# A two-layer recurrent-memory transformer on one core: sums and value products in column tiles, and an order for each of four segments

## The chip, the core and the metric

The kernel runs on one core of a Trainium2 chip. The metric is the device time of the whole launch in microseconds (us). TensorE is called PE here, VectorE DVE, ScalarE ACT, GpSimd POOL, SyncE SP. PE multiplies a loaded (stationary) block of weights with a moving operand. It can be used as one array of 128 x 128 ("full") or as four column tiles of 128 x 32 that work on outputs in four groups of 32 partitions ("col"). A row of the profile that says `128*128` is a full matmul, one that says `128*32` a matmul in one column tile. PE writes to eight PSUM banks, from which ACT and DVE copy results out.

## The reference

The input has 2048 tokens of width 512. Two kinds of layer alternate, A B A B, each on a layer norm (LN) of the running sum and added to it.

```python
def _A_ref(x, mem0, Wq, Wk, Wv, Wo, seg_len):        # 32 heads of 128, seg_len 32, M = 8
    mem = mem0
    for s in range(n_seg):                            # 64 segments, one after the other
        h = concatenate([mem, x[:, s*seg_len:(s+1)*seg_len]], axis=1)     # 40 rows
        q, k, v = h @ Wq, h @ Wk, h @ Wv              # per head
        p = softmax(where(mask, q @ k.T * scale, -1e9))
        o = (p @ v) @ Wo                              # summed over heads
        mem = o[:, :M]                                # goes into the next segment
        outs.append(o[:, M:])

def _B_ref(x, wqkv, wo):                              # 32 heads of 16, linear attention
    q, k, v = split(x @ wqkv)
    pq, pk = phi(q), phi(k)                           # phi(t) = t+1 or exp(t), + 1e-6
    kv, z = pk.T @ v, sum(pk)                         # over all 2048 tokens
    return ((pq @ kv) / (pq @ z + 1e-6)) @ wo
```

The `mask` is causal among the tokens of a segment; its first eight columns, the memory, are seen by all rows.

## The kernel before, in words

**Tiling.** The tokens are 16 tiles of 128 rows; a tile has four segments of 32 tokens. For each segment (`a_layer`, the loop over `s` from L1190) the operand `hT` holds 8 memory rows and 24 of the 32 tokens, so a block has 32 columns and fits a column tile. The last eight tokens of each segment ("left") are gathered for the four segments of a tile and projected together, once a tile (`left_block`, L857). `project` (L786) makes half of the 32 heads at a time: four k-blocks, each with four matmuls in the four column tiles, 512 columns each. The halves are called b = 0 and b = 1. Keys and queries are then turned by transposes on PE (L815) or by a DMA transpose on SP's queue (L806).

**One segment.** In order: keys, queries and values for both halves; scores of the memory queries and all others (`mem_attention`, L916: L936 and L942), Exp on ACT (L953), a masking product on DVE (L963), the sums over keys (L969: a matmul with ones, so that every partition gets the sum), the inverse of the sum as Exp of -Ln (L972, L974), the products with values (L979 for the left keys, L982 for the others), the scaling on DVE (L986). Then `out_block` projects with Wo (L1084), and `next_mem` (L1109) makes the next segment's memory rows. That loop is the recurrence. The attention of the segment's own tokens (`x_attention`, L991: sums at L1014 and L1018, products with values at L1050 and L1054) needn't be finished for the next memory; its output joins the next segment's output projection.

**Layer B** runs beside it: `b_in` (L1236) takes a finished tile's LN (transposes at L764), projects (L1246, L1280) and accumulates kv and z (L1258, L1264); `b_mid` combines them with the output weights; `b_out` (L1327) applies them (L1349, L1357), while the second A layer runs, and once more at the end. `prepare` (L905) makes the LN of the next tile for layer A.

**Modes before.** Projections, transposes of keys and queries, scores, L1014, L1018, L1084 and L1109 are `mode="col"`. L969, L979, L982, L1050, L1054 and the matmuls of layer B and of LN have `mode="full"`, the default of `add`.

**What sets the order.** The program is a list of nodes; `schedule` (L221) walks a modelled time and gives each engine its next node, so every engine's instruction order is fixed when the kernel is built. Semaphore waits follow from the dependencies. A node's priority comes from a written table, OFFSET, by the name of its step and its number in it:

```python
nd.prio = -(step * PERIOD + OFFSET[name][k])
```

Here `step` is the segment number. The higher priority goes first. On PE the mode counts too (L344 to L353): the node of highest priority is set aside in favour of a ready node of the present mode, unless that one's priority is lower by more than MODE_SLACK; a switch is charged PE_SWITCH = 0.1 us in the plan. LOOK (L356) lets PE hold back when a node of higher priority becomes ready within that time. A node that is not urgent also has to leave PSUM banks free for urgent ones.

The function `at` (L780) names the step: the plain name for most segments, with `F` at the first of a layer and `L` at the end. `c_pe` and `c_pe4` (L110 to L115) are the plan's costs of full and of column matmuls.

Of the kernel before, what the change touches and what calls it, by code (L numbers as in the profile page):

```python
# [19 lines left out]
MODE_SLACK = 257.520800  # L20

LOOK = 0.037900

PERIOD = 13.5
# [6 lines left out]
    "startF": (-180.90,),  # L31
    "prepF": (-121.35, 60.85, -338.25, -337.90, -107.00, -87.50, -299.25, -329.00, -408.50, 3.85, -143.55),
    "left0F": (-363.40, -329.55, -494.35, -352.10, 94.85, -208.40, -136.40, -396.90, -232.20, -403.00, -128.90,
        -405.80, -148.00, -295.50),
    "left1F": (-209.80, -257.05, -186.90, -154.30, -433.85, 6.40, -172.20, -140.25, -80.85, -9.85, -9.35, -386.50,
        -138.50, 95.25),
    "leftv0F": (-372.65, -364.30, -359.05, -256.70, -165.10, -31.45, -453.65, -169.80, -349.15),
    "leftv1F": (11.05, -371.15, -43.60, -159.70, -312.30, -127.00, -348.85, -412.35, -37.50),
    "leftsF": (152.10, -203.75, -335.15, -313.60),
    "xlF": (-408.90,),  # L40
    "k0F": (-374.05, -352.95, -109.35, -38.25, -357.80, -283.65, -389.25),
    "k1F": (-384.40, -311.20, -269.15, -445.45, -358.65, -231.45, 6.45),
    "q0F": (-231.35, -263.70, -41.50, -77.50, -422.45, -255.85, -244.15),
    "q1F": (-403.90, -236.15, -154.40, -217.85, -201.95, 40.05, -395.10),
    "v0F": (-150.70, -57.40, -88.00, -91.90, -412.95),
    "v1F": (-398.50, -281.20, -428.10, -152.00, -135.45),
    "qlF": (-276.35, -262.00),
    "mem0F": (144.85, -273.95, -326.25, -10.00, -100.65, -352.15, -184.30, -65.00, -152.00, -199.90),
    "mem1F": (143.65, -361.45, -383.05, -187.15, -362.20, -392.75, -272.00, -305.00, -257.25, -132.25),
    "warm": (-58.15,),  # L50
    "outF": (-106.90, -344.50, -302.90, -95.35, -235.60, -405.55, -256.55, -367.55, -76.60, -394.15),
    "nextF": (-363.25, 27.95, -353.90),
    "xF": (-185.90, -377.55, 14.75, -293.55, -309.80, -426.90, -378.30, 31.70, -109.50, -293.25, -82.35, -367.45,
        -244.60, -240.60, -354.70, -77.85, -232.55, -363.15, -367.00, -361.35, 25.20, -367.30, 44.65),
    "k0": (-398.40, -409.05, -373.85, -369.85, 132.45, -419.80),
    "k1": (-365.35, -358.40, -356.75, -359.10, -107.85, -297.25, -150.20),
    "q0": (-362.10, -361.85, -360.10, -360.10, -210.50, -303.20, -149.75),
    "q1": (-355.65, -305.05, -346.50, -363.20, -182.55, -219.85, -25.65),
    "v0": (-95.30, 11.05, -162.10, -296.90, -355.00),
    "v1": (-86.30, -164.30, -100.90, 16.15, -110.55),  # L60
    "ql": (-65.10, 8.65),
    "mem0": (-95.60, -319.85, -382.80, -364.30, -364.60, -238.25, -382.75, -409.25, -242.75, -363.50),
    "mem1": (-383.00, -337.30, -215.20, -155.05, -146.75, -237.10, -384.30, 73.95, -107.50, -247.10),
    "out": (-133.90, -320.25, -243.80, -151.90, -140.55, -192.85, -130.00, -224.85, -109.70, -359.70),
    "next": (-146.50, -384.40, -71.35),
    "res": (-183.00, 64.70, -297.70, -251.95, -411.00, -412.55, -365.55, -304.60, -304.65, -295.30, -246.05,
        -110.55, -74.25, -19.80, -371.90),
    "x": (-109.05, -31.75, 114.50, -203.10, -411.65, -359.40, -250.75, -429.60, -384.75, -272.75, -52.30, -225.80,
        -224.30, -229.40, -102.00, -5.70, 33.60, -84.35, -151.60, -296.60, -389.35, -9.55, -276.50),
    "prep": (-19.30, -365.40, -305.25, -166.00, -378.25, -251.70, -384.90, -194.75, -380.20, -282.75, 77.85),  # L70
    "left0": (32.80, -324.50, -411.15, -307.75, -358.90, -202.25, -79.65, -207.35, -187.55, -161.70, -154.90,
        -304.30, -258.10),
    "left1": (-122.95, -119.30, -37.50, -257.65, 25.80, 45.20, -304.15, -368.35, -295.60, -220.55, -372.95,
        -155.60, -281.60),
    "leftv0": (-150.60, -87.70, -74.05, -89.65, 87.70, -306.35, -427.50, 74.20),
    "leftv1": (-93.05, -335.75, -148.00, -153.60, -355.55, -48.40, 175.80, -359.40),
    "lefts": (15.65, -231.70, -259.75, -320.50),
    "xl": (-368.40,),
    "bi": (-160.30, -165.65, -384.40, -460.85, -352.00, -423.00, -276.75, -132.25, -251.60, -360.20, -121.05,
        -144.60, -284.90, -386.70, -405.60, 165.25, -301.95, -305.30, -356.70, -156.05, -73.25, -115.15, 25.75,  # L80
        37.60, -11.70, -163.20, 100.35, -134.80, -166.80, -114.00, -147.35, -398.65),
    "k0L": (-245.45, -353.50, -300.20, -334.30, -361.55, -384.65, -370.40),
    "k1L": (-342.20, -303.05, -383.70, -269.65, -361.15, -244.35, -335.50),
    "lr": (-341.45, -312.30, -306.75, -164.75, -284.05, -386.00, -357.55, -334.15, -416.50, 161.80, -67.40,
        -334.55, -56.15),
    "xL": (154.80, -139.25, -428.60, -145.30, -313.00, -200.15, -368.90, -369.95, -367.85, -432.15, -360.25, 65.65,
        -193.75, -336.60, -371.50, -220.70, -310.95, -427.55, -78.15, -373.70, -404.65),
    "outL": (-183.35, -223.20, -247.40, -365.15, -74.00, -380.60, -56.90, -223.50, -345.60, -38.20),
    "resL": (-280.85, -402.40),
    "biL": (-330.50, -308.55, -333.35, -91.15, -389.95, -228.15, -76.30, -32.45, -294.50, -121.05, -167.60,  # L90
        -377.75, -262.40, -270.20, -25.45, -14.60, -313.50, 59.95, -373.25, -319.65, -43.90, -426.45, -404.80,
        159.50, 90.55, -275.05, -114.60, -274.80, -0.20, -245.85, -186.45, -160.00),
    "bm": (-410.80, -480.25, -344.35, -394.70, -170.00, -356.70, -6.85, 40.95, -34.25, 28.70, -27.10, -86.70, 81.00),
    "boF": (-189.35, -384.50, -486.20, -152.40, -345.90, -400.30, -157.90, -333.20, -255.25, -380.60, -218.45),
    "bo": (-354.35, -361.60, -26.00, -195.25, -364.05, -132.50, 137.45, -348.35, -267.60, -258.70, -358.25),
    "ldL": (-68.35, -367.55),
    "boL": (-254.80, -187.90, -323.40, -61.20, -302.90, -321.15, -73.00, -462.70, -32.35, -155.00),
    "boZ": (-401.60, -128.20, -116.30, -62.60, -31.35, -177.45, -365.75, -28.05, -77.75, -79.45),
# [15 lines left out]
def c_pe(n_mm, n):  # L114
    return n_mm * max(0.0335, (n / 2.4 + 3.0) * 1e-3)  # L115
# [390 lines left out]
def _build_kernel(nc, A_x, A_mem0, A_Wq, A_Wk, A_Wv, A_Wo, A_seg_len, B_wqkv, B_wo, out):  # L506
# [110 lines left out]
    add = P.add  # L617
# [156 lines left out]
    LATE = ("x", "k0", "k1")  # L774

    def a_layer(base, first):
# [3 lines left out]
        def at(s, name):  # L780

            early = s <= 0 or (name[:4] == "left" and not by_dma(s))
            P.at(base + s, name + ("F" if early else "L" if s >= NSEG or (s == NSEG - 1 and name in LATE) else ""))
# [132 lines left out]
        def mem_attention(s, b):  # L916
# [50 lines left out]
            def sums(pe):  # L967
                for a in range(2):
                    r = pe.matmul(tl.f32()[:, 256:384], one_sb[:, :], Pm[:, k, a, :], start=(a == 0), stop=(a == 1))  # L969
                return r  # L970
            add("pe", sums, c_pe(2, 128), reads=[("Pm", k, 0), ("Pm", k, 1), "one"], tiles=[tl], urgent=True)
# [6 lines left out]
            def pvm(pe):  # L978
                pe.matmul(pv.f32()[:, 0:128], vleft[:, g2, b, g, :], Pm[:, k, 1, :], start=True, stop=False)  # L979
                for i, hh in enumerate(hhs):  # L980
                    o = slice(32 * i, 32 * i + 32)
                    r = pe.matmul(pv.f32()[:, o], vimg[:, r2, 128 * hh:128 * hh + 128], Pm[:, k, 0, o], start=False,  # L982
                                  stop=i == 3)
                return r
            add("pe", pvm, c_pe(4, 32) + c_pe(1, 128), reads=[("Pm", k, 0), ("Pm", k, 1), ("v", r2, b), ("vl", g2, b)], tiles=[pv], urgent=True)
# [5 lines left out]
        def x_attention(s):  # L991
# [50 lines left out]
            for b in range(2):  # L1042
                pv = P.tile()
                for i in range(4):

                    def pvx(pe, i=i, b=b, pv=pv):
                        hh = 4 * b + i
                        o = pv.f32()[:, 128 * i:128 * i + 128].rearrange("p (j q) -> p j q", j=4)
                        e = slice(128 * hh, 128 * hh + 128)
                        r = pe.matmul(o, vimg[:, r2, e], Pbx[:, hh, :, :], start=i == 0, stop=False,  # L1050
                                      skip_group_check=True)
                        if i == 3:
                            o = pv.f32()[:, :].rearrange("p (n q) -> p n q", q=32)[:, :, 24:32]
                            r = pe.matmul(o, vleft[:, g2, b, g, :], Pbl[:, b, :], start=False, stop=True,  # L1054
                                          skip_group_check=True)
# [363 lines left out]
```

## Time and profile before

| | us |
|---|---|
| median of 3 runs | 1759.76 |
| lowest, highest | 1757.05, 1760.36 |
| the profiled execution's own time | 1759.18 |
| its span, first to last instruction | 1757.0 |
| PE busy (matmuls) | 1671.6 |
| PE weight loads busy | 1098.7 |
| DVE busy | 1133.8 |
| ACT busy | 1130.2 |
| POOL busy | 329.3 |

The mean granted clock of PE was 0.993 of full speed. In the timeline's rows, the first column is the start from the beginning of the span, the second the time from the first start to the last end of the group, then engine, line, what is written and read, weights and moving operand, and the number of instructions. In brackets is the idle time before it and what ended that. Matmuls overlap: a row's duration contains the latency of its last matmul, so the pace of PE is read from one start to the next. In the list of waits the numbers are total us, times, and the longest.

### The profile page before, as it was taken

How to read it: one execution, taken by the hardware profiler on the slowest of the kernel's cores; microseconds unless marked ns; L12 is line 12 of the kernel's file. 1: busy time of each engine (PE TensorE's matmuls, PEld its weight loads, DVE VectorE, ACT ScalarE, POOL GpSimd, SP SyncE). 2: the span in 40 equal slices, each digit the busy share in tenths (PEclk: the TensorE clock that was granted, in tenths of full speed). 3: DMA queues.
4: the chain of work that ended last, by engine and by line, in shares of the span. 5: the costliest groups of instructions: out<-in, count | busy, mean ns of one | idle time of the engine just before them, and what ended most of it. 6: DMA issues, size and time to landing. Idle time of an engine off the chain costs nothing.

```text
span 1757.0 us, 101000 instructions
## 1 busy us (share of the span) xinstructions
PE 1671.6 (95%) x46027; PEld 1098.7 (63%) x46027; DVE 1133.8 (65%) x3960; ACT 1130.2 (64%) x3069; POOL 329.3 (19%) x660
## 2 busy tenths in 40 slices
PE   5999999999999999999799999999999999999997
PEld 2666666666666666666466666666666666666663
DVE  2566666666666666666555666667666766666657
ACT  3666666666666666666466666666666666666665
POOL 2022221112221111222102221122221112221120
PEclk9999999999999999999999999999999999999999
DMA  9222222212222222222012222122222222222223
GB/s 378 77 37 45 46 45 43 50 39 46 45 41 46 45 47 40 47 50 39 22 25 40 47 47 54 36 52 48 42 52 48 42 45 48 47 47 48 51 68 105
DMA packets 228540, 97.47 MB, mean 55 GB/s; under 512 B 207096, under 2 KB 222256, under 8 KB 226576
## 3 DMA queue, kind: packets, MB, share of 16 engines
q1 hardware_dynamic: 204784, 58.64, 17.8%
q0 software_dynamic: 21744, 19.78, 5.1%
q10 hardware_dynamic: 1584, 12.58, 1.7%
q8 instruction: 360, 5.90, 1.4%
q14 instruction: 68, 0.56, 0.1%
HBM read 29.63 MB, written 10.49 MB: 23 GB/s over the span
## 4 chain that ended last, share of the span: by engine, by line
PE 80%; DMA 8%; DVE 5%; ACT 5%; issue 1%; POOL 1%; ACTq 0%; DVEq 0%
PE pb L793 42%; PE pb L1084 14%; PE pb L815 4%; PE pb L1050 4%; DMA arena_sb<-arena_sb 4%; PE pb L1246 3%; DMA dx_sb<-y_sb 2%; PE pb L936 2%; DVE arena_sb L623 2%; PE pb L1280 2%; PE pb L969 1%; ACT arena_sb L622 1%; DMA Wk_sb<-in_A_Wk_dram 1%; PE pb L1109 1%; PE pb L764 1%
## 5 line engine op out<-in xcount | busy, mean ns | idle before, releaser
L622 ACT ACTIVATE arena_sb<-pb 128x512 bf16<-128x512 f32 (+6 forms) x1375 | 674.3, 509 | 302.6 <-PE pb L793 223.4
L638 POOL DMA_DIRECT2D dx_sb<-y_sb x504 | 256.8, 516 | 1095.6 <-DVE y_sb L1120 485.0
L793 PE MATMUL pb<-Wk_sb,arena_sb 128*32 128x512 bf16 x5120 | 346.7, 382 | 16.5 <-DVE arena_sb L623 6.5
L793 PE MATMUL pb<-Wv_sb,arena_sb 128*32 128x512 bf16 x5120 | 354.0, 379 | 1.7 <-issue 1.6
L793 PE MATMUL pb<-Wq_sb,arena_sb 128*32 128x512 bf16 x5120 | 340.0, 381 | 0.5 <-DMA Wq_sb<-in_A_Wq_dram 0.5
L1084 PE MATMUL pb<-Wo_sb,arena_sb 128*32 128x256 bf16 x10368 | 329.5, 273 | 9.9 <-DVE arena_sb L986 8.8
L1084 PEld LDWEIGHTS pb<-Wo_sb,arena_sb 128*32 128x32 bf16 x10368 | 265.8, 97 | 42.4 <-DVE arena_sb L986 20.3
L623 DVE CAST arena_sb<-pb 128x512 bf16<-128x512 f32 (+3 forms) x459 | 232.7, 519 | 83.8 <-PE pb L793 66.0
L623 DVE COPY arena_sb<-pb 128x512 bf16<-128x512 bf16 (+2 forms) x422 | 150.5, 365 | 172.7 <-PE pb L815 156.9
L623 DVE COPY arena_sb<-arena_sb 32x256 bf16<-32x256 bf16 (+2 forms) x960 | 202.3, 211 | 72.4 <-PE pb L942 18.8
L793 PEld LDWEIGHTS pb<-Wk_sb,arena_sb 128*32 128x32 bf16 x5120 | 131.9, 97 | 122.0 <-DVE arena_sb L623 8.9
L793 PEld LDWEIGHTS pb<-Wq_sb,arena_sb 128*32 128x32 bf16 x5120 | 131.9, 97 | 116.5 <-issue 2.1
L622 ACT ACTIVATE outW_sb<-pb 128x128 fp32r<-128x128 f32 x288 | 79.8, 277 | 158.3 <-PE pb L1084 153.9
L793 PEld LDWEIGHTS pb<-Wv_sb,arena_sb 128*32 128x32 bf16 x5120 | 115.7, 95 | 48.4 <-issue 2.6
L815 PEld LDWEIGHTS pb<-id_sb,arena_sb 128*32 128x32 bf16 x6304 | 110.5, 97 | 53.6 <-DVE arena_sb L623 12.1
L953 ACT ACTIVATE arena_sb<-pb 128x192 bf16<-128x192 f32 (+1 forms) x256 | 81.6, 329 | 93.2 <-PE pb L942 47.8
L815 PE MATMUL pb<-id_sb,arena_sb 128*32 128x128 bf16 x6304 | 135.7, 219 | 0.1
L1120 DVE TENSOR_TENSOR y_sb<-pb,outW_sb 64x256 bf16<-64x256 f32 x158 | 65.8, 417 | 87.1 <-ACT outW_sb L622 84.4
L1050 PE MATMUL pb<-arena_sb 128*128 128x128 bf16 x1024 | 114.0, 220 | 5.5 <-DVE arena_sb L623 4.2
L963 DVE TENSOR_TENSOR arena_sb<-arena_sb 128x128 bf16<-128x128 bf16 x504 | 86.4, 220 | 16.8 <-ACT arena_sb L953 15.7
L1050 PEld LDWEIGHTS pb<-arena_sb 128*128 128x128 bf16 x1024 | 69.4, 97 | 40.8 <-issue 19.3
L986 DVE TENSOR_TENSOR arena_sb<-pb,arena_sb 128x128 bf16<-128x128 f32 x252 | 68.0, 286 | 25.7 <-ACT arena_sb L974 15.6
(123 smaller groups left out, 1962.5 us busy)
## 6 DMA issues: line engine op xcount, KB each, us to landing
arena_sb<-arena_sb SPq DMA_TRANSPOSE x356, 2.8
Wq_sb<-in_A_Wq_dram ACTq DMA_DIRECT2D x1, 4096.0 KB, 13.6
Wk_sb<-in_A_Wk_dram ACTq DMA_DIRECT2D x1, 4096.0 KB, 24.5
Wv_sb<-in_A_Wv_dram ACTq DMA_DIRECT2D x1, 4096.0 KB, 35.0
Wo_sb<-in_A_Wo_dram SPq DMA_DIRECT2D x4, 1024.0 KB, 11.7
xs_scratch<-x_sb POOLq DMA_DIRECT2D x32, 128.0 KB, 2.0
pq_scratch<-arena_sb POOLq DMA_DIRECT2D x32, 128.0 KB, 2.5
dx_sb<-y_sb POOLq DMA_DIRECT2D x252, 12.0 KB, 2.0
```

The lines of the kernel that those rows point to most:

```text
L622: return e.activation(o() if callable(o) else o, i() if callable(i) else i, ACTF.Copy)
L623: return e.tensor_copy(o() if callable(o) else o, i() if callable(i) else i)
L638: add(eng, lambda e: e.dma_start(o, i), 0.55 if eng == "pool" else 0.4, reads=reads, writes=writes, dsem="%s%d" % (kind, k), lat=lat + (0. ...
L793: r = pe.matmul(tl.f32()[32 * j:32 * j + 32, 0:512], blk[:, c, :], W[:, c, o:o + 512], start=(c == 0), stop=(c == 3), tile_position=(0, 32 ...
L815: r = pe.transpose(tt.bf16()[32 * j:32 * j + 32, 128 * i:128 * i + 128], img[:, k, o:o + 32], id_sb[:, :], tile_position=(0, 32 * j))
L953: add("act", lambda a: a.activation(PQ[:, r2, b, 0:nq], tl.f32()[:, 0:nq], ACTF.Exp, scale=SCALE), c_act(nq), tiles=[tl], writes=[("PQ", r ...
L963: add("dve", lambda v, a=a, p_=p_, w_=w_: v.tensor_tensor(wide(Pm[:, k, a, :]), p_.unsqueeze(2).to_broadcast([128, 4, 4, 8]), w_, ALU.mult ...
L986: add("dve", lambda v: v.tensor_tensor(oTb[:, s % NO, 16 * b:16 * b + 16, 0:8], pv.f32()[:, 0:128].rearrange("p (n q) -> p n q", q=8), Rm[ ...
L1050: r = pe.matmul(o, vimg[:, r2, e], Pbx[:, hh, :, :], start=i == 0, stop=False, skip_group_check=True)
L1084: r = pe.matmul(tl.f32()[32 * j:32 * j + 32, 0:256], oT[:, 4 * hh + n, :], Wo_sb[:, 8 * n + hh, 256 * d:256 * d + 256], start=(hh == 0 and ...
L1120: add("dve", lambda v: v.tensor_tensor(y_sb[0:64, k, :], tl.f32()[0:64, 0:256], outW[64:128, w, :].bitcast(F32), ALU.add), c_dve(256), rea ...
L1246: add("pe", lambda pe, c=c: pe.matmul(dst.f32()[:, :], xlnT[:, c, :], wqkv_sb[:, c, o:o + D], start=(c == 0), stop=(c == 3)), c_pe(1, 512) ...
```

## The change

It has two parts.

1. The matmuls of L969, L979, L982, L1050 and L1054 are written as four matmuls of 32 weight columns in the four column tiles, each with the same moving operand as before and a quarter of the output's partitions. Their nodes become `mode="col"`, with `c_pe4` as their cost in the plan.
2. The order. For the names in EACH, the plain name is replaced by one of four, by the segment's place in its tile (`s % 4`), each with offsets of its own. All of OFFSET is new; PERIOD, MODE_SLACK and LOOK change.

```diff
-MODE_SLACK = 257.520800
-LOOK = 0.037900
-PERIOD = 13.5
+MODE_SLACK = 1.707500
+LOOK = 0.000000
+PERIOD = 12.815
 OFFSET = {
...
-    "k0": (-398.40, -409.05, -373.85, -369.85, 132.45, -419.80),
+    "k0b": (-3.35, -19.35, -48.00, -43.40, 8.80, -43.00),
...
+    "k0c": (-29.10, -62.10, -31.30, -28.75, -4.40, -30.00),
...
+    "k0d": (-24.65, -24.60, -23.70, -33.20, 36.90, -9.20),
...
+    "k0a": (-27.05, -26.00, -23.75, -22.75, 0.30, -36.05),
...
+    EACH = ("k0", "k1", "q0", "q1", "v0", "v1", "ql", "mem0", "mem1", "out", "next", "res", "x")
...
-            P.at(base + s, name + ("F" if early else "L" if s >= NSEG or (s == NSEG - 1 and name in LATE) else ""))
+            P.at(base + s, name + ("F" if early else "L" if s >= NSEG or (s == NSEG - 1 and name in LATE) else
+                                   "abcd"[s % 4] if name in EACH else ""))
...
                 for a in range(2):
-                    r = pe.matmul(tl.f32()[:, 256:384], one_sb[:, :], Pm[:, k, a, :], start=(a == 0), stop=(a == 1))
+                    for j in range(4):
+                        q = slice(32 * j, 32 * j + 32)
+                        r = pe.matmul(tl.f32()[q, 256:384], one_sb[:, q], Pm[:, k, a, :], start=(a == 0), stop=(a == 1),
+                                      tile_position=(0, 32 * j))
                 return r
-            add("pe", sums, c_pe(2, 128), reads=[("Pm", k, 0), ("Pm", k, 1), "one"], tiles=[tl], urgent=True)
+            add("pe", sums, c_pe4(8, 128), reads=[("Pm", k, 0), ("Pm", k, 1), "one"], tiles=[tl], urgent=True, mode="col")
...
             def pvm(pe):
-                pe.matmul(pv.f32()[:, 0:128], vleft[:, g2, b, g, :], Pm[:, k, 1, :], start=True, stop=False)
+                for j in range(4):
+                    q = slice(32 * j, 32 * j + 32)
+                    pe.matmul(pv.f32()[q, 0:128], vleft[:, g2, b, g, q], Pm[:, k, 1, :], start=True, stop=False,
+                              tile_position=(0, 32 * j))
                 for i, hh in enumerate(hhs):
                     o = slice(32 * i, 32 * i + 32)
-                    r = pe.matmul(pv.f32()[:, o], vimg[:, r2, 128 * hh:128 * hh + 128], Pm[:, k, 0, o], start=False,
-                                  stop=i == 3)
+                    for j in range(4):
+                        e = 128 * hh + 32 * j
+                        r = pe.matmul(pv.f32()[32 * j:32 * j + 32, o], vimg[:, r2, e:e + 32], Pm[:, k, 0, o], start=False,
+                                      stop=i == 3, tile_position=(0, 32 * j))
                 return r
...
-                        r = pe.matmul(o, vimg[:, r2, e], Pbx[:, hh, :, :], start=i == 0, stop=False,
-                                      skip_group_check=True)
+                        for c in range(4):
+                            q = slice(32 * c, 32 * c + 32)
+                            e = 128 * hh + 32 * c
+                            r = pe.matmul(o[q], vimg[:, r2, e:e + 32], Pbx[:, hh, :, :], start=i == 0, stop=False,
+                                          skip_group_check=True, tile_position=(0, 32 * c))
...
-                    add("pe", pvx, c_pe(1 + i // 3, 128),
+                    add("pe", pvx, c_pe4(4 + 4 * (i // 3), 128), mode="col",
```

The left part of `pvx` (L1054) and the cost of `pvm` change in the same manner. `k0` stands for the 13 names in EACH.

## The prediction

> **What bounds the kernel now.** I read the page first: which engine is full, and who carries the chain that ended last.
>
> ```profile
> PE 1671.6 (95%) x46027; PEld 1098.7 (63%) x46027; DVE 1133.8 (65%) x3960; ACT 1130.2 (64%) x3069; POOL 329.3 (19%) x660
> ...
> PE   5999999999999999999799999999999999999997
> ...
> PE 80%; DMA 8%; DVE 5%; ACT 5%; issue 1%; POOL 1%; ACTq 0%; DVEq 0%
> ```
>
> PE is at nine tenths or more in every slice but the start, the border between the layers and the end; ACT and DVE are at two thirds. But a matmul's listed duration is latency, so I went to the timeline of PE and read start to start.
>
> ```profile
> 812.50 0.41 PE L815 MATMUL pb<-id_sb,arena_sb 128*32 128x128 bf16 x16
> 812.72 0.40 PE L793 MATMUL pb<-Wv_sb,arena_sb 128*32 128x512 bf16 x4
> 812.94 0.20 PE L942 MATMUL pb<-arena_sb 128*32 128x32 bf16 x4
> ...
> 813.53 0.27 PE L936 MATMUL pb<-arena_sb 128*32 128x40 bf16 x16
> 813.63 1.26 PE L793 MATMUL pb<-Wv_sb,arena_sb 128*32 128x512 bf16 x20
> 814.82 0.40 PE L969 MATMUL pb<-arena_sb,one_sb 128*128 128x128 bf16 x4
> 815.14 0.29 PE L1018 MATMUL pb<-arena_sb,bo_sb 128*32 128x256 bf16 x4
> 815.26 0.20 PE L1014 MATMUL pb<-arena_sb,bo_sb 128*32 128x64 bf16 x4
> 815.40 0.23 PE L979 MATMUL pb<-arena_sb 128*128 128x128 bf16 x1
> 815.47 0.26 PE L982 MATMUL pb<-arena_sb 128*128 128x32 bf16 x4
> 815.68 0.23 PE L979 MATMUL pb<-arena_sb 128*128 128x128 bf16 x1
> 815.74 0.25 PE L982 MATMUL pb<-arena_sb 128*128 128x32 bf16 x4
> 816.29 0.40 PE L1084 MATMUL pb<-Wo_sb,arena_sb 128*32 128x256 bf16 x8 [0.29 <-DVE arena_sb L986]
> ```
>
> A pack of four column tiles (128*32) with 512 columns takes 0.216 us; sixteen transposes of L815 take 812.72 - 812.50 = 0.22, so 0.055 a pack; sixteen of L936 take 0.10, so 0.025 a pack. Of full-array matmuls (128*128), those with 128 columns start 0.056 apart and those with 32 columns 0.025 apart. Twenty of L793 need 5 x 0.216 = 1.08, from 813.63 to 814.71, and L969 starts at 814.82: entering full mode cost 0.11. The last two rows are the way back: four of L982 end at 815.84 and L1084 starts at 816.29; 0.29 of that 0.45 is a named wait for the scaled product (L986), which stands at the border but isn't the drain.
>
> I took all 46027 start-to-start intervals of the trace and subtracted this pace from each. The span of 1757.0 us is then 1557.4 of pace, 6.0 before the first and after the last start, and 193.7 of excess: 60.2 at the entries into full mode, 41.0 at the exits, 92.5 between matmuls of one mode. There are 261 visits to full mode. The cheap tenth of the entries costs 0.118 and a typical exit 0.093, so a bare visit is 0.211 us, 55 in all. About 65 of the excess lies outside the steady stretches (0 to 52 us, 845 to 905, 1698 to the end). In the steady stretches (124 segments) it is 128.8: 243 visits x 0.211 = 51.3 bare, and 77.5 of waits.
>
> Is it instead the recurrence from one segment's memory to the next? Starts of L1109, one group per segment, lie 12.81 us apart on average in layer one and 13.02 in layer two, and the shortest interval is 10.79. The pace alone is 724.7 / 62 = 11.7 us a segment in layer one and 732.3 / 62 = 11.8 in layer two. So the chain can run faster than PE's work allows: PE's work, its visits and its waits set the time. The waits of PE that the trace names are small and many:
>
> ```profile
> PE pb L1084 <- DVE arena_sb L986: 8.8, 33, 0.7
> PE pb L793 <- DVE arena_sb L623: 6.5, 19, 0.4
> PE pb L936 <- DMA arena_sb<-arena_sb: 6.4, 12, 1.2
> ...
> PE pb L1050 <- DVE arena_sb L623: 4.2, 18, 1.0
> ```
>
> **What the Trainium skill says.** TensorEngine Tiling (Array Packing), Tiling Modes: changing the tiling mode, not just the tile, drains TensorE; the trace has 0.118 in and 0.093 out. The same page, under Restrictions, says column tiling disables fast weight load; yet the trace lists 97 ns for loads of 128x32 as of 128x128, and four loads with their matmuls fit in 0.055 (L815) and 0.025 us (L936), so it doesn't bind here. TensorE: Matmul & The Clock Gate, Part 1, gives N/2.4 GHz plus about 2.5 ns between starts, 55.6 ns at 128 columns and a floor of about 25 ns; the trace agrees. Its Part 3 says matmuls in distinct column tiles run concurrently; the packs show it.
>
> **The change, part by part.**
>
> *Matmuls.* L969 (504), L979 (252), L982 (1008), L1050 (1024) and L1054 (256) each become four of 32 columns: 3044 to 12176, so 9132 more matmuls and as many loads. Before: 2036 x 0.056 + 1008 x 0.025 = 139 us. After: 2036 packs x 0.055 + 1008 x 0.025 = 137. I take 0. The closest row is L815, which has the same form as the new matmuls: four different weight slices against one moving operand. The upper bound, if a pack had to pay the 97 ns of one load, is 2036 x 0.041 + 1008 x 0.072 = +156; L815 and L936 exclude it, and I keep +10 for long dense stretches. One semaphore per group as before. Instruction fetch grows by 18264 on 101000, on a queue at 1.4% of the DMA engines.
>
> *Visits.* All changed groups leave full mode. By the order of PE's matmuls, 87 of the 261 visits hold nothing else (32 are L979 L982 L979 L982, 26 are L1050 L1054 L1050 L1054, 20 are L969 alone). These go: 87 x 0.211 = -18.4. At their borders lie 22.1 + 19.2 = 41.3 of excess, so 22.9 of waits stand there too: sums waiting for the masked scores (L963), products waiting for copies (L623), the output projection behind the product's scaling (L986). Once no drain separates them, projections can fill these waits: -22.9, with a bound of 0 if they merely move. The other 174 visits keep LN transposes and layer B work and stay.
>
> *Order.* MODE_SLACK falls from 257.5 to 1.7: before, PE kept its mode as long as anything of that mode was ready within 257 us of priority, some nineteen periods; now it switches when the other mode is ahead by 1.7. Beforehand, work of the recurrence in one mode could stand behind any ready work in the other. Afterwards the recurrence (projections, transposes, scores, sums, products, output, next memory) is one mode and meets full mode only at layer B and LN. Each of four segments also gets its own offsets, so the segment with LN and left projections ahead (mean interval 13.4 us) need not share an order with a light one (12.3). What this is worth no row shows. Of the steady waits, 77.5 - 22.9 = 54.6 remain. The lower bound of the gain is below nothing, since an order can also make waits (rival 4 prices one way); the upper bound is all 54.6. I take a third, -18: work to fill them with is there (six left projections per four segments), but many of them are a latency that an order can't remove, such as the output projection behind the product's scaling. What is late next is an evacuation: ACT and DVE are 65% busy, with the copies of L622 and L623 behind most matmul groups.
>
> *Switching more often.* Visits may rise. Planned separately, layer B and LN have at most 32 x 15 (input side) + 32 x 5 (output side) + 32 (prepare) + about 20 = 690 nodes in full mode. Each extra visit costs 0.211 bare. I take 174; the least I see is about 160 (four visits per tile in layer one, six in layer two), -3.
>
> *Queues.* No DMA is added or removed, but all instructions are reordered: SP's 356 transposes (2.8 us to landing) and POOL's moves of dx, xs and pq. PE waited only 6.4 us on those transposes. One tenth of a microsecond late at each of the 126 on the recurrence would be +13; that is in the range. POOL's moves end in the residual add (DVE L1161), four segments ahead of layer B, and no PE wait names them in the steady part. Start, layer border and end are chains through LN, ACT and DVE (2.74 us before L764, 2.27 before L1357); I take 0 and keep 8 either way.
>
> PERIOD falls from 13.5 to 12.815, but it only scales the due times that priorities are made of, and before's own mean interval in layer one is 12.81 already: it says nothing on the pace after. LOOK matters only within 0.04 us: 0.
>
> Sum against the profiled span: 1757.0 - 18.4 - 22.9 - 18 = 1697.7. The profiled run took 1759.18, 2.2 above its span, and the median is 1759.76, another 0.6: 1700.5, so 1700 us, 3.4% faster.
>
> **Rivals.**
>
> 1. Forecast: the pure visits go with the waits at their borders, and part of the other waits. 1665 to 1730, **chance 0.54**.
> 2. The waits nearly vanish: 18.4 + 77.5 + 3 + 8 = 107 off gives 1650 on the span, 1653 as a median. For: 11.7 us of pace leaves room, and the chain has done 10.79. Against: evacuations on engines that are 65% busy. 1650 to 1665, **chance 0.10**.
> 3. Only the tiles count and the order is neutral: 1757 + 2.8 less 18.4 to 41.3 gives 1718 to 1741. For: PE is already kept busy, and the named waits are small. From 1730 to 1756, as the order may lose a little too, **chance 0.17**.
> 4. The smaller slack scatters layer B: its projections (L1246) and feature products (L1280) get visits of their own between column work, each 0.211. The gain forecast, 59.3, is used up at 59.3 / 0.211 = 281 more visits, 455 in all; 500 visits give 1769, and 600 give 1700.5 + 426 x 0.211 = 1790. For: 690 nodes would allow it, and 1.7 us of slack hardly holds a mode together. Against: layer B's nodes become ready in groups behind one transposed LN tile, and 455 is 14 visits a tile where 4 to 6 would do. **Slower, chance 0.14**.
> 5. Gain and scattering cancel to within 0.2%: **chance 0.05**.
>
> A difference under about 0.2% can't be told from none with these times. Faster is 0.54 + 0.10 + 0.17 = 0.81, same 0.05, slower 0.14. For 8 in 10, the range from 1655 to 1756 leaves out about half of case 2 and nearly all of cases 4 and 5 (0.05 + 0.15); the likeliest case's own range is 1665 to 1730.
>
> **What would show it.** Right: near 55160 matmuls; the changed lines as 128*32, with packs of 128 columns 0.056 us apart; visits near 174 (150 to 220); pace unchanged at about 1557; excess down from 194 to about 134; mean intervals of L1109 near 12.3 and 12.55 us. Wrong in the matmuls: packs above 0.07. Wrong in the visits: over 300. Wrong in the waits: new waits of PE on copies, or on SP's transposes, above 20 us for one pair of lines. The forecast fails outright if the new order starves PE behind evacuations, which no row of before can show.

## The result, and the profile after

The kernel after takes 1840.1 us (median of 4 runs, 1837.45 to 1843.33) beside 1758.4 us for the kernel before: a ratio of 1.0465, 95% interval 1.0441 to 1.0488. It is slower by 82 us where I had forecast 3.4% faster. The profiled execution took 1837.45 us, its span is 1835.3, so 78.3 us above the span before. From the page of the kernel after (busy time, the instruction queue, the chain that ended last; line numbers have moved by about 40: L831 is L793 of the kernel before, L974 is L936, L1009 is L969, L1098 is L1050, L1134 is L1084):

```profile
span 1835.3 us, 118977 instructions
...
PE 1689.6 (92%) x55077; PEld 1128.8 (62%) x55159; DVE 1111.3 (61%) x3779; ACT 1165.5 (64%) x3250; POOL 327.4 (18%) x660
...
q8 instruction: 431, 7.06, 1.6%
...
PE 66%; DMA 15%; ACT 8%; DVE 7%; issue 4%; POOL 0%; ACTq 0%; DVEq 0%
```

From the page of the kernel before, the row to set beside the third:

```profile
q8 instruction: 360, 5.90, 1.4%
```

PE's share of the chain fell from 80% to 66%, DMA's rose from 8% to 15%, and "issue", time in which the engine waited for nothing that the profile shows, from 1% to 4%. ACT is busy 35 us longer than before and DVE 22 us less, and neither is fuller: 64% and 61% of the span, beside 64% and 65%. All but 82 of the 55159 matmuls have a record. The number of fetches on the instruction queue rose from 360 to 431, each of 16384 bytes: 92054 PE instructions (matmuls and loads) over 360 and 110318 over 431 are both 256 to a fetch.

The timeline of PE in the kernel after at three places (start, length, line, operation, and in brackets the idle time before it and what ended it); the middle one has the new column packs:

```profile
302.00 0.29 PE L1134 MATMUL pb<-Wo_sb,arena_sb 128*32 128x256 bf16 x3
302.81 1.39 PE L1134 MATMUL pb<-Wo_sb,arena_sb 128*32 128x256 bf16 x44 [0.52 <-issue]
...
803.24 0.28 PE L1009 MATMUL pb<-arena_sb,one_sb 128*32 128x128 bf16 x8
803.36 0.39 PE L831 MATMUL pb<-Wv_sb,arena_sb 128*32 128x512 bf16 x4
803.57 0.28 PE L1009 MATMUL pb<-arena_sb,one_sb 128*32 128x128 bf16 x8
803.68 0.28 PE L1064 MATMUL pb<-arena_sb,bo_sb 128*32 128x256 bf16 x4
...
1241.38 0.40 PE L831 MATMUL pb<-Wv_sb,arena_sb 128*32 128x512 bf16 x3
1242.87 1.47 PE L831 MATMUL pb<-Wv_sb,arena_sb 128*32 128x512 bf16 x21 [1.09 <-issue]
```

Eight matmuls of the sums (L1009), two packs, take 0.11 to 0.12 us: the packs have the pace that I forecast, 0.056. But PE stops in the middle of an output projection, after three matmuls of a pack of four, and goes on 0.81 us later; and again in a value projection, 1.49 us from one start to the next. The fourth matmul of a pack needs nothing that the third did not need; in the first case its weights had even been loaded, at 302.01 us, and only the matmul itself came late. The waits of PE after:

```profile
PE pb L974 <- DMA arena_sb<-arena_sb: 20.0, 23, 2.1
PE pb L800 <- DVE arena_sb L794: 16.0, 5, 9.0
PE pb L1134 <- issue: 10.3, 17, 1.3
...
PE pb L1098 <- issue: 6.3, 12, 0.9
...
PE pb L831 <- issue: 5.2, 8, 1.1
```

Before, the largest wait of this kind was

```profile
PE pb L793 <- issue: 1.6, 2, 1.1
```

and all of them together were 3.8 us, beside 38 now. So two things are new: waits for nothing named, and the wait of the scores (L974, before L936) for the transposed keys, 6.4 us before and 20.0 now.

I then laid the landings of the fetches on the instruction queue beside PE's gaps (a gap is what lies between two starts beyond the pace of the first). In the kernel after, 94 gaps of 0.25 us or more end 1.2 to 1.6 us after a fetch has landed, 68.6 us in all; before there are 30, 19.7 us. That gave the theories for the experiments. A: instruction supply, dense runs of small matmuls use up 256 instructions faster than the next fetch comes. B: the new order makes waits. C: the column form of these lines is slow in itself. Below, "fetch waits" are gaps over 0.15 us that end 1 to 2 us after a landing: 60 gaps and 32.6 us before, 163 and 101.4 after. As fetches land every 4 us or so, about a quarter of any gaps fall into that window by chance.

A sharper count needs no such window. If the supply is the cause, PE must stop where one fetched block of 256 instructions ends and the next begins, so at the same place in every 256. I numbered PE's instructions by its weight loads (they all have a record; two for each load with its matmul, and one for each recorded semaphore instruction) and took every interval over 0.25 us between successive starts of loads and matmuls. In the kernel after, 86 of 450 such intervals, 58.2 us, stand at one place of the block (numbers 193 and 194 of 256), where chance would put three. In the kernel before, 8 of 345 stand there, 5.8 us. I call them edge stops. Of the kernels in this document six have more than twelve of them, and the place is the same in all six.

### The profile page after: what moved, and what is told of

Read it like the earlier page. It is cut to its first block, busy times and chain, and to the rows that moved or that the text cites. A ratio compares the mean times of both kernels' runs of the same rounds, so it can differ in the third digit from the quotient of the medians.

```text
span 1835.3 us, 118977 instructions
## 1 busy us (share of the span) xinstructions
PE 1689.6 (92%) x55077; PEld 1128.8 (62%) x55159; DVE 1111.3 (61%) x3779; ACT 1165.5 (64%) x3250; POOL 327.4 (18%) x660
## 4 chain that ended last, share of the span: by engine, by line
PE 66%; DMA 15%; ACT 8%; DVE 7%; issue 4%; POOL 0%; ACTq 0%; DVEq 0%
PE pb L831 34%; DMA arena_sb<-arena_sb 12%; PE pb L1134 12%; PE pb L853 3%; PE pb L1098 3%; ACT arena_sb L658 3%; PE pb L1296 3%; DVE arena_sb L659 2%; PE pb L974 2%; DMA Wk_sb<-in_A_Wk_dram 1%; PE pb L1159 1%; PE pb L1009 1%; DVE arena_sb L1001 1%; PE pb L1022 1%; PE pb L1028 1%
## 5 line engine op out<-in xcount | busy, mean ns | idle before, releaser
L831 PE MATMUL pb<-Wv_sb,arena_sb 128*32 128x512 bf16 x5120 | 384.9, 379 | 4.3 <-issue 4.2
L831 PE MATMUL pb<-Wk_sb,arena_sb 128*32 128x512 bf16 x5120 | 375.0, 381 | 12.7 <-ACT arena_sb L658 7.2
L831 PE MATMUL pb<-Wq_sb,arena_sb 128*32 128x512 bf16 x5120 | 374.4, 381 | 2.2 <-issue 1.0
L1134 PE MATMUL pb<-Wo_sb,arena_sb 128*32 128x256 bf16 x10368 | 340.9, 273 | 12.7 <-issue 10.3
L1134 PEld LDWEIGHTS pb<-Wo_sb,arena_sb 128*32 128x32 bf16 x10368 | 269.1, 97 | 55.4 <-issue 18.7
L659 DVE COPY arena_sb<-arena_sb 32x256 bf16<-32x256 bf16 (+2 forms) x834 | 177.6, 214 | 141.7 <-DMA arena_sb<-arena_sb 84.6
L658 ACT ACTIVATE outW_sb<-pb 128x128 fp32r<-128x128 f32 x319 | 88.6, 278 | 201.3 <-PE pb L1134 161.0
L831 PEld LDWEIGHTS pb<-Wq_sb,arena_sb 128*32 128x32 bf16 x5120 | 145.6, 97 | 103.2 <-issue 6.5
L831 PEld LDWEIGHTS pb<-Wk_sb,arena_sb 128*32 128x32 bf16 x5120 | 142.8, 97 | 106.4 <-ACT arena_sb L658 10.0
L831 PEld LDWEIGHTS pb<-Wv_sb,arena_sb 128*32 128x32 bf16 x5120 | 120.2, 95 | 39.1 <-issue 8.2
L1098 PE MATMUL pb<-arena_sb 128*32 128x128 bf16 x4096 | 119.8, 219 | 9.7 <-issue 6.3
L1098 PEld LDWEIGHTS pb<-arena_sb 128*32 128x32 bf16 x4096 | 84.4, 96 | 41.3 <-DVE arena_sb L659 19.2
```

Of the source, the lines that this page charges most:

```text
L658: return e.activation(o() if callable(o) else o, i() if callable(i) else i, ACTF.Copy)
L659: return e.tensor_copy(o() if callable(o) else o, i() if callable(i) else i)
L831: r = pe.matmul(tl.f32()[32 * j:32 * j + 32, 0:512], blk[:, c, :], W[:, c, o:o + 512], start=(c == 0), stop=(c == 3), tile_position=(0, 32 ...
L1098: r = pe.matmul(o[q], vimg[:, r2, e:e + 32], Pbx[:, hh, :, :], start=i == 0, stop=False, skip_group_check=True, tile_position=(0, 32 * c))
L1134: r = pe.matmul(tl.f32()[32 * j:32 * j + 32, 0:256], oT[:, 4 * hh + n, :], Wo_sb[:, 8 * n + hh, 256 * d:256 * d + 256], start=(hh == 0 and ...
```

## The experiments

### The old order with column tiles, the new order with the full array

Each engine's instruction order stays exactly as it was in one of the two kernels, and only the form of the five lines is exchanged: the plan is given the modes and costs that belong to the order, the matmuls are issued in the other form. For the old order, for instance (the last line, which the plan reads, stays as in the kernel before):

```diff
             def sums(pe):
                 for a in range(2):
-                    r = pe.matmul(tl.f32()[:, 256:384], one_sb[:, :], Pm[:, k, a, :], start=(a == 0), stop=(a == 1))
+                    for j in range(4):
+                        q = slice(32 * j, 32 * j + 32)
+                        r = pe.matmul(tl.f32()[q, 256:384], one_sb[:, q], Pm[:, k, a, :], start=(a == 0), stop=(a == 1),
+                                      tile_position=(0, 32 * j))
                 return r
             add("pe", sums, c_pe(2, 128), reads=[("Pm", k, 0), ("Pm", k, 1), "one"], tiles=[tl], urgent=True)
```

> Every engine's instruction order is exactly that of the kernel before; only the five matmul lines are issued as column tiles (the plan keeps their old modes and costs, so nothing is reordered). Theory A (instruction supply: PE's instructions arrive in fetches of 16 KB, 256 instructions, and dense runs of small column matmuls use them up faster than the next fetch lands): 9132 more matmuls and loads cost 30 to 60 us of unnamed PE waits that end shortly after a fetch; full-mode visits fall from 261 to 218, worth -9. Sum 1780 to 1810 us. Theory B (the new order is the cause, the column form is free): about 1749, -9 from the visits and up to -20 of waits at their borders.

> Every engine's instruction order is exactly that of the kernel after; only the five matmul lines are issued on the full array (the plan keeps the new modes and costs). Full-mode visits rise from 204 to 520, which costs 316 x 0.211 = +67 us. Theory A (instruction supply): 18264 fewer PE instructions take about 60 to 70 us of fetch waits away, so the sum stays near 1840 (1825 to 1855), with the waits that end after a fetch back at the level of before. Theory B (order alone): no such waits to lose, 1840 + 67 = 1907 us.

Old order, column tiles: 1834.65 us, 1.0429 (1.0409 to 1.0448) times the kernel before. New order, full array: 1832.29 us, 1.0424 (1.0403 to 1.0444). In numbers of the profiled executions, with the median time last (visits are counted from the weight loads, which all have a record, and can be one or two above the counts in the expectations):

| kernel | matmuls | visits to full mode | fetches | fetch waits: times, us | edge stops: times, us | median us |
|---|---|---|---|---|---|---|
| before | 46027 | 261 | 360 | 60, 32.6 | 8, 5.8 | 1758.67 |
| old order, column tiles | 55159 | 218 | 431 | 163, 91.9 | 100, 67.2 | 1834.65 |
| after | 55159 | 206 | 431 | 163, 101.4 | 86, 58.2 | 1840.1 |
| new order, full array | 46027 | 501 | 360 | 75, 47.2 | 10, 6.5 | 1832.29 |

The page and the waits of the old order with column tiles:

```profile
span 1831.6 us, 119264 instructions
...
q8 instruction: 431, 7.06, 1.6%
```

```profile
PE pb L936 <- DMA arena_sb<-arena_sb: 12.7, 22, 1.2
PE pb L1096 <- issue: 12.5, 26, 1.7
PE pb L1096 <- DVE arena_sb L994: 8.2, 30, 0.7
...
PE pb L1060 <- issue: 5.1, 7, 1.6
```

The first run rules out B as the cause of the loss: with no instruction moved, the column form costs 76 us, and the time lies above even the 1780 to 1810 us of theory A. Between A and C it does not decide alone, but that the stops keep their place in the block speaks for A. L1096 is the output projection (L1084 before), whose own form did not change, and its largest wait now is "issue". The pace is the same, 1557.4 us in both. Of the 74.6 us by which the profiled span grew, 61.4 are edge stops, close to the 59.3 of the wider window. If all the time at the edge is taken, short intervals too, beyond the mean of the other places of a block, it is 5.5 us before and 79.0 here: 73.5 of the 74.6. The borders of full mode did become cheaper, from 101.2 us of excess to 67.4. But within a mode the excess rose by 108.3 us, 35 more than the edges take: what was saved at the borders came back as other waits.

The kernel after and the old order with column tiles have the same forms and differ only in order: 1.0465 and 1.0429 times the kernel before, with intervals that overlap. In that form the new order is no gain. New order with the full array shows the other side: 18264 fewer instructions take nearly all edge stops away, and 295 more visits give the time back. Its excess at the borders is 174.1 us, and within a mode it is 93.0, as before the change (92.5).

### Each half of the change as the planner makes it

Here the planner gets the new modes with the old table, or the old modes with the new table, so that the order changes too.

> The column form with its new modes and costs in the plan, but the old table of offsets, slack 257.5 and period. The old table was made for a recurrence that crosses both modes. Theory A: the fetch waits of the kernel after are there too (about 100 us in waits that end after a fetch), 1840 to 1920 us. Theory B: 1740 to 1760 us.

> The new table, slack 1.7, period and the four orders per tile, with full-array matmuls planned as such. Theory A: fetch waits at the level of before (about 33 us), but the recurrence crosses modes with almost no slack: over 500 full-mode visits, +60 us and the waits on drains in the chain; 1850 to 1920 us. Theory B: also slow, above 1840, as the order is what costs; the count of waits that end after a fetch tells the two apart: near 60 in both only if they come from instruction count.

They took 1870.91 and 1928.02 us (one execution each), beside 1758.67 for the kernel before. Their fetch waits are 151 gaps with 73.5 us and 103 with 61.4, with so many gaps of other kinds in either that the chance share is large. The edge stops tell them apart: 58 with 37.8 us for the column form, 12 with 10.1 us for the full array, so they go with the form under this order too. The rest of the loss is other waits. It shows that a table fits one set of modes: with the other set, both are slower than either whole kernel, and neither half of the change can be judged by leaving out the other.

### More instructions without any change of form

To separate A from C, the matmuls of the scores, which were column tiles all along, are issued three times over in the kernel before.

```diff
                 for i, hh in enumerate(hhs):
-                    for j in range(4):
-                        r = pe.matmul(tl.f32()[32 * j:32 * j + 32, 40 * i:40 * i + 40], kT[:, hh, j, :],
-                                      qT[:, hh, j, :], start=True, stop=True, tile_position=(0, 32 * j))
+                    for again in range(3):
+                        for j in range(4):
+                            r = pe.matmul(tl.f32()[32 * j:32 * j + 32, 40 * i:40 * i + 40], kT[:, hh, j, :],
+                                          qT[:, hh, j, :], start=True, stop=True, tile_position=(0, 32 * j))
```

> The kernel before, with the score matmuls of L936 issued three times over (the same operands into the same place, so the result stays as it is): 8192 more matmuls and as many loads, no matmul changes its form and no mode switch is added. At the pace of 0.025 us for a pack of four this is 2048 x 0.025 = +51 us of TensorE work by itself. Theory A (instruction supply): another 40 to 80 us come on top, most of it in waits that end 1.2 to 1.6 us after an instruction fetch has landed, so 1850 to 1890 us. Theory C (the column form of the five changed lines is slow in itself, by its loads or drains, and fetches only happen to lie near): nothing on top, about 1810 us.

1910.95 us, 1.0847 (1.0826 to 1.0868): 150 us more, above the range of theory A. From the timeline of this kernel:

```profile
810.09 0.61 PE L937 MATMUL pb<-arena_sb 128*32 128x40 bf16 x48
810.52 0.21 PE L943 MATMUL pb<-arena_sb 128*32 128x32 bf16 x4
810.55 0.61 PE L937 MATMUL pb<-arena_sb 128*32 128x40 bf16 x46
812.48 0.20 PE L937 MATMUL pb<-arena_sb 128*32 128x40 bf16 x2 [1.31 <-issue]
```

Forty-eight score matmuls take 0.43 us here (median 0.417), about 0.035 a pack and not the 0.025 of four packs alone. So the work itself is about 0.32 us more for each of 256 groups, some 81 us, where I had expected 51. Here is the plainest picture of a wait, too: 46 of 48 matmuls that read only keys and queries that are there already, and the last two start 1.93 us after the first, where 0.4 would do. The fetch waits are 146 gaps with 116.5 us, 84 more than before; the edge stops are 78 with 87.1 us, 81 more. (The two sums together exceed 150 us; by subtraction, other waits got some 10 us shorter.) No line changed its form and no switch was added, so theory C is not needed; 8192 more small matmuls in dense runs, of a form that was there all along, bring the same waits at the same place of the block.

### Choosing the form group by group

Can a mixed form win? The order stays, and where a group of matmuls can be issued either way (LN transposes, sums, both value products, layer B's rows and output products) a pass over PE's list chooses the form, at a price for each turn between the modes and for each added instruction.

In the code, `f` is 0 for full and 1 for column, and `n_mm` is the group's number of full matmuls (0.3 for those of 512 columns):

```diff
+            own = [INF if only_col else 0.0, INF if only_full else 6 * nd.n_mm * INSTR]
...
+            for f in range(2):
+                stay, turn = best[f], best[1 - f] + SWITCH
...
+                now.append(min(stay, turn) + own[f])
```

> The order of the kernel before, instruction by instruction. For each group of matmuls that can be issued either way (LN transposes, sums, both value products, layer B's rows and output products) the form is chosen by the groups beside it: column tiles where that saves a visit to full mode for few added instructions. Visits 261 to 131; about 2800 dense and some hundred sparse matmuls more. Theory A: -130 x 0.211 = -27 (up to -50 with the waits at their borders), and + 6000 instructions at 2.6 to 4.6 ns = +16 to +28: 1730 to 1760 us. Theory C: column matmuls of the changed lines cost about 85 us / 9132 each, 2800 of them +26: about the same sum, so this run doesn't tell A from C; it tells whether a mixed form beats the kernel before.

> The order of the kernel after, instruction by instruction, with the form of each such group chosen in the same way: visits 129 (204 in the kernel after, 500 with all of them full), about 4300 matmuls more than all full where the kernel after has 9132 more. Theory A: from the kernel after, -75 x 0.211 = -16 and half of the supply waits, -40: about 1785 us. Theory B (order): 1840 - 16 = 1824 us.

Old order: 1768.4 us, 1.0042 (1.0027 to 1.0058), with 48967 matmuls and 132 visits, fetch waits 46.4 us. New order: 1797.29 us, 1.0212 (1.0172 to 1.0253), with 50470 matmuls and 130 visits, fetch waits 55.2 us. So about half of the loss goes when half of the added instructions go, in the new order too. There the edge stops are 31 with 21.1 us, in the old order 31 with 22.5. Both times lie above what theory A had expected. With the old order, half of all visits were removed and nothing was gained. The time rose by 7 us and the edge stops by 17, so 129 fewer visits brought about 10 us and not the 27 that I had expected. That contradicts the price of a visit, so I varied it:

> The order of the kernel before; forms chosen in both directions, now also key and query transposes (L815) and the sums of the segment's own tokens (L1014, L1018) as full-array matmuls where that saves more instructions than the drains cost. About 3100 matmuls fewer than before (6200 instructions with their loads), visits 261 to 318. Prices fitted to the runs so far: 0.0089 us per added matmul with its load, 0.18 us per visit. Theory A (instruction supply): -3133 x 0.0089 + 57 x 0.18 = -18: about 1741 us. Drains alone (no price on instructions): +10, about 1769 us.

> The same with a dearer switch: as many matmuls as before (-139) and visits 261 to 193. Theory A with the fitted prices: -1 - 68 x 0.18 = -13: about 1746 us. If waits at the borders go with the visits, up to -27: 1732 us. If a visit's drain only covers a wait that stands there anyway, no change: 1759 us.

With 43003 matmuls and 319 visits: 1776.68 us, 1.0096 (1.0077 to 1.0116), fetch waits 31.2 us. With 45997 matmuls and 194 visits: 1759.06 us, 1.0002 (0.9990 to 1.0013), fetch waits 35.1 us. Both expectations of A failed, in its prices. Fewer instructions than before bring nothing: at the level of before the supply is hardly a limit, fetch waits stay at 31 to 35 us, which is about what chance would put there, and there are 6 edge stops in either run. And a visit has no fixed price in these runs: with 58 more visits the time is 17 us longer, but 67 fewer bring nothing. In that last run the excess at entries and exits is 88.6 us (101.2 before) and the excess within a mode 105.3 (92.5 before): the drains went, and waits of the same length in sum stood in their place. Its page and waits:

```profile
span 1758.1 us, 100940 instructions
```

```profile
PE pb L1173 <- DVE arena_sb L1054: 9.7, 34, 0.6
PE pb L985 <- DMA arena_sb<-arena_sb: 6.9, 14, 1.2
```

L1173 is the output projection, L1054 the scaling of the product that it waits for; before, this pair stood at 8.8 us and 33 times. The output projection waits for the same operand as before, with fewer drains ahead of it.

## Why the prediction was wrong, by its own steps

**Matmuls ("I take 0").** This is the step that failed. The pace of the packs was right, 0.055 to 0.06 us. The bound of +156 that I excluded came from weight loads, and they don't bind. What I had priced at nothing in one sentence, "Instruction fetch grows by 18264 on 101000, on a queue at 1.4% of the DMA engines", was the cost: the old order with column tiles measured +76 us, at least 61 of them in stops at the edge of a fetched block. The share of a queue says nothing of it. In all kernels with 424 to 431 fetches, no two of them start closer than 3.24 to 3.30 us, so 256 instructions each 3.25 us are the most that arrived here, 13 ns each. Before, 8% of all windows of 128 load and matmul pairs are passed in under 3.3 us; after, 19%; in the old order with column tiles 24%. I should have divided: a pack of four transposes of L815 is eight instructions in 0.055 us, 7 ns each, twice that rate. This was harmless as long as such runs were short and stood between projections of 27 ns an instruction. The change adds 72 matmuls with their loads to most segments, in its densest places.

**Visits (-18.4) and the waits at their borders (-22.9).** Of the 261 visits, 87 do hold nothing but changed groups. But in 44 others a changed group stands between two pieces of other full work, and these split in two, so the old order keeps 261 - 87 + 44 = 218 visits and not 174: 43 fewer, 9 us at my own price. That the kernel after has 206, inside the 150 to 220 that I named, is luck. (Rival 4, scattering, did not occur.) The gain did not come either. In the old order with column tiles the borders lost 33.8 us of excess and other waits gained 35; with 67 fewer visits alone the time did not move (1.0002). My bound of 0 for the border waits, "if they merely move", is what happened, and there it holds for the drains as well. In the new order the price held better: the full array there has 295 more visits and 52 us less of edge stops, and is 8 us faster, so a visit cost some 0.15 us, an estimate from these two kernels. I had read 10.79 us, the shortest interval of the memory step, as proof that the recurrence is not the limit. It shows only that one interval can be short; in a fixed order, the waits for the scaled product and the transposed keys stay.

**Order (-18).** With equal forms the new order brought nothing that can be measured (1.0465 and 1.0429 times the kernel before). Scores waited 20.0, 16.7 and 19.6 us for the keys' DMA transposes in the three kernels with the new order and its own table (after, full array, chosen form), against 6.4 and 5.8 in the old order (before, chosen form) and 12.7 with its column tiles. So the wait comes partly with the order and partly with the column form. I had put +13 for it into the range as a possibility, and took 0.

**Pace.** Right where it can be read: 1557.4 us in the old order with column tiles, as before. In the kernel after, 82 missing records leave 1539.7.

**The rivals.** The slower rival named the wrong mechanism. Slower by an instruction supply was not on the list, and the only place that touched it was a percentage of a queue. The +10 that I kept "for long dense stretches" was the right thought with an eighth of the size.

What stays open: why a visit that is added costs time in the old order and one that is removed gives none back; how much of the new order's wait for transposed keys is the order's own; and whether an order made with the supply in its costs would win with column tiles. No kernel tried here beats the kernel before.

## What to carry to other kernels

Splitting a full matmul into column tiles left its time on the array here and multiplied its instructions by four. Ahead of such a change, count instructions (with loads) per microsecond in the densest microsecond or two of the engine and compare them with the tightest spacing of the instruction fetches in the trace, not with the queue's share. To see whether the supply binds, number the engine's instructions: stops by the supply keep one place in each fetched block. And a removed drain or bubble on a busy engine is a gain only if the next thing in a fixed order is ready; exchange the form with the order held still, and the order with the form held still, before believing either.

## What the runs showed of the hardware that I had not expected

- PE's instructions came in fetches of 16384 bytes for 256 instructions, never started closer than 3.22 us to each other in any kernel here. A fetch's own transfer took 1.0 to 1.1 us (median).
- In the old order with column tiles, the fetch that a stopped block waited for had started 1.1 us (median) after the block before it began, and the stop ended 1.4 us after that fetch had landed (1.2 to 1.6 in nine of ten). No block there began less than 1.19 us after its fetch had landed.
- So it is quick blocks that end in a stop: of 126 blocks that PE ran through in under 3.25 us, 74 were followed by one, of 177 that took over 4 us, two. The kernel before has 25 such quick blocks in all.
- These waits have no releaser in the profile: they appear as "issue", often in the middle of a pack, and partly on rows that are not dense at all, since the fetch boundary falls where it falls.
- Sixteen small column matmuls in a row start 6 ns apart (0.10 us for L936), forty-eight 9 ns apart (0.43 us): in the longer burst, a load and its matmul take 9 ns.
